# Softcap attention and a max-out feed-forward on one core: a new order of work up to the ninth quad, and hand-overs placed anew

## The chip, the core and the metric

The kernel runs on one core of a Trainium2 chip. The metric is the device time of one execution in microseconds (us), given as the median of several runs. The engines that matter are TensorE (PE, with its weight loads as PEld), VectorE (DVE), ScalarE (ACT), GpSimd (POOL) and SyncE (SP). Each engine takes its instructions one after the other from its own queue and meets the others by semaphores. Here POOL issues most of the loads, SP the stores and the transposing loads, so a wait on one of these queues holds back the transfers that are queued behind it.

## The reference

```python
# q, k, v: (8, 12, 448, 64) float32; cap = 30
scores = scale * np.matmul(q, k.transpose(0, 1, 3, 2))   # scale = 1/8
scores = cap * np.tanh(scores / cap)
attn = softmax(scores)
x = (attn @ v).transpose(0, 2, 1, 3).reshape(3584, 768)
# w1, w2: (768, 1024); w_out: (1024, 768)
h1 = x @ w1
h2 = x @ w2
out = np.maximum(h1, h2) @ w_out                          # (3584, 768) float32
```

Each of 8 batches has 12 heads over 448 tokens. The scores are squeezed by a tanh, made into weights by an exponential and a division by their sum, and applied to the values. The result, heads side by side, is the input of a feed-forward layer that takes the larger of two projections.

## The kernel before

**What is computed where.** A *pair* is two heads, a *quad* t is the pairs 2t and 2t+1; there are 24 quads, three to a batch. All products are in bf16. For each pair PE computes the scores, keys by queries, in three steps of 128 keys (`S i j`, line 514) into one of two PSUM tiles that are used in turn; the 64 keys that remain of each head are done for a quad at once (`L t`, line 528). ACT takes the tanh out of PSUM (`T i j`, line 519; `TL t`, line 532) and later the exponential in SBUF (`E i j0 j1`, line 536; `EL t`, line 539). Since tanh bounds the scores by 30, no maximum is subtracted. The sums over keys are made by PE with a matrix of ones (`Y t`, lines 566, 570 and 573); from the fourth quad on DVE first adds the key blocks (`A`, line 548, and `B`, line 553), so that PE has fewer matmuls to do. DVE inverts the sums (`Y1`, `Y2`, `Y3`, lines 578, 581, 584), PE applies the values (`VL t`, line 600, for the leftover keys, which opens the sum, then `V t u j0 j1`, line 606), which land in a score tile too, and DVE multiplies by the inverse and writes the input of the layer, `xT` (`N t u`, lines 618 and 621).

**The layer.** The larger of two projections is x·w2 + relu(x·(w1−w2)). So the kernel forms wd = w1−w2 once (`sub c e`, line 402, on DVE or POOL) and wm = w2·w_out once: PE transposes w2 (`W`, line 416, copied out by `WC`, line 420) and multiplies (`OP c half bank` opens a sum in a bank, `P c half n` adds n of its 8 matmuls, line 431, `PC` copies it out on DVE, line 437). Then every stage 1 group computes gT = relu(wd·x) for 128 of the 1024 columns of one batch, and every stage 2 group x·wm + gT·w_out for 128 tokens and half of the 768 columns, in 14 units. There are 120 groups. `O g bank` opens one in one of four PSUM banks; a unit is a matmul of 128 rows, done as two half matmuls of 64 rows that may run beside each other in the upper and the lower half of PE's rows. `M x y n` issues n pairs: the upper half of group x's next unit and the lower half of group y's (line 645). So a group is finished in two spells, one in each row half, and neighbouring groups overlap.

**Hand-overs.** Both halves of a group add into the same bank. When a group goes from one row half to the other, the first matmul there waits for a nop, which itself waits for the group's last matmul in the first half: `H g` puts the nop on DVE, `Hs g` on SP (line 654). As DVE and SP are queues, what stands behind such a nop waits with it. Of 145 such passes in the kernel before, 107 have a nop on SP, 21 one on DVE and 17 none.

**Evictions and stores.** `ev g` empties a finished group on DVE (relu at line 666, copy at line 702), `eva g` does the copy on ACT (line 700); `st b t` stores on SP (lines 676 to 681, 705 to 707).

**Loads and transposes.** `ld0` and `cd` load and cast the first pair's rows; `lk`, `lq`, `lv`, `lw1`, `lw2`, `lwo` are loads issued by POOL that cast on the way (lines 321, 328, 352, 393, 366, 360). The first ten pairs are transposed by PE (`X i bank`, `Xh`, line 458, copied by `XC`, line 463), the later quads by a transposing transfer issued by SP (`cr t`, line 475). `D bank n` is a filler matmul on PE while nothing else can run (line 471).

**What sets the order.** The program is one list of steps, `ORDER`, written out from line 9 on; a loop at the end calls each step's function, and the instructions go to their engines in this sequence. Nothing is rescheduled: moving a step in the list moves its instructions on its engine past the others of that engine.

```python
for s in ORDER.split(";"):
    if s.strip():
        name, *args = s.split()
        STEPS[name](*[int(a) if a.lstrip("-").isdigit() else a for a in args])
```

Of the kernel before, what the change touches and what calls it, by code (L numbers as in the profile page):

```python
# [24 lines left out]
OP 5 1 3; P 5 1 4; S 6 2; L 3; Y 2 1; T 6 2; TL 3; E 6 0 3; VL 2; V 2 1 0 1; V 2 0 0 3; V 2 1 1 3; S 7 0; P 5 1 4;
OP 5 0 0; P 5 0 8; Y1 2; Y2 2; Y3 2; N 2 0; N 2 1; A 3 0 1; A 3 0 2; PC 5 1; PC 5 0; T 7 0; EL 3; lk 9 0; lq 11 0;
lv 3 1; lq 9 0; lw1 1; lw1 3; lq 10 0; lk 12 1; lv 3 0; lw1 5; lk 10 0; lk 11 0; lk 11 1; lk 10 1; S 7 2; O 0 1;
M 0 -1 2; S 7 1; M 0 -1 4; O 1 2; M 1 -1 1; T 7 2; T 7 1; Hs 0; M 1 -1 1; S 8 1; M 1 -1 1; M 1 0 3; S 8 0; X 9 3;
OP 4 1 0; P 4 1 4; sub 1 0; sub 3 0; XC 9; T 8 1; E 7 0 2; T 8 0; E 7 2 3; P 4 1 4; L 4; O 2 3; M 2 0 3; S 8 2;
M 2 1 3; A 3 1 1; B 3 1; PC 4 1; ev 0; B 3 0; Hs 2; TL 4; T 8 2; O 3 0; M 3 1 3; M 3 2 1; S 9 0; M 3 2 2; T 9 0;  # L30
E 8 0 3; ev 1; A 3 1 2; sub 5 0; cr 5; Hs 3; O 4 1; M 4 2 1; VL 3; V 3 0 0 3; Y 3 2; V 3 1 0 3; M 4 2 2; S 9 1;
M 4 3 3; lk 13 0; lk 13 1; lv 4 1; lv 4 0; lv 5 3; lv 5 0; lq 13 0; lq 15 0; lq 12 0; lk 12 0; lk 15 1; Y1 3;
Y2 3; Y3 3; ev 2; Hs 4; O 5 2; M 5 3 3; M 5 4 3; T 9 1; EL 4; ev 3; N 3 0; N 3 1; Hs 5; O 6 3; M 6 4 3; M 6 5 2;
S 10 0; M 6 5 1; O 7 0; M 7 5 3; Hs 6; ev 4; A 4 0 1; ev 5; M 7 6 2; S 9 2; M 7 6 1; Hs 7; cr 6; E 9 0 2; T 10 0;
T 9 2; O 8 1; M 8 6 3; S 10 2; M 8 7 3; S 10 1; O 9 2; M 9 7 1; T 10 2; T 10 1; E 9 2 3; M 9 7 2; VL 4; V 4 0 0 2;
L 5; TL 5; A 4 1 1; H 8; A 4 0 2; B 4 1; ev 7; B 4 0; A 4 1 2; ev 6; M 9 8 3; V 4 1 0 3; Y 4 0; V 4 0 2 3;
M 9 8 7; S 11 0; M 9 8 1; O 10 3; M 10 8 3; E 10 0 3; T 11 0; EL 5; Hs 9; Hs 8 2; Y1 4; M 10 9 3; Y2 4; Y3 4;
N 4 1; N 4 0; M 8 9 2; S 11 1; M 8 9 3; S 11 2; M 8 9 3; lv 5 2; lk 15 0; lk 14 0; lv 6 1; lk 14 1; lq 14 0;
lv 5 1; lq 16 0; lv 6 3; lv 6 0; lk 16 1; lk 17 0; lk 16 0; T 11 1; T 11 2; E 11 0 2; O 11 0; M 11 9 3; S 12 0;
M 11 10 6; S 12 1; M 11 10 1; ev 8; ev 9; A 5 0 1; A 5 0 2; lk 17 1; M 11 10 4; T 12 0; lq 17 0; O 12 1;  # L40
M 12 10 1; A 5 1 1; M 12 10 1; Hs 11; cr 7; M 12 10 1; M 12 11 1; B 5 0; M 12 11 1; T 12 1; M 12 11 1; S 12 2;
# [164 lines left out]
def kernel(  # L206
# [21 lines left out]
    P = 128  # L228
# [550 lines left out]
```

## Time and profile before

| what | value |
|---|---|
| median of 3 runs | 328.49 us (328.19 to 328.52) |
| span of the profiled execution | 326.9 us |
| time of the profiled execution beside its span | not given on the page; the median lies 1.59 us above the span |
| PE busy | 320.2 us, 98%, 4138 matmuls |
| ACT busy | 281.1 us, 86%, 278 instructions |
| DVE busy | 240.1 us, 73%, 422 instructions |
| POOL busy | 162.2 us, 50% |
| chain that ended last | PE 93%, DMA 3%, POOL 1%, DVE 1% |

The span runs from the first to the last instruction of the profiled execution. Busy time of an engine counts every moment in which one of its instructions is under way; matmuls overlap, so that a PE that is busy all the time may still start its matmuls further apart than it could. The chain of waits is followed back from the last instruction. In a row of a group the name at the left of the arrow is what is written and at the right what is read; behind x stands the count, then the busy time and the mean length of one in ns, then the idle time ahead of them and what ended it. In a row of a timeline stand the start, the length, the engine, the line and the number of instructions that were merged into the row.

### The profile page before, as it was taken

Reading aid. Unit: us, or ns where it says so; the run is one execution under the profiler, and the core shown is the slowest. Engines: PE = TensorE matmul, PEld = TensorE weight load, DVE = VectorE, ACT = ScalarE, POOL = GpSimd, SP = SyncE. Lnnn points to the kernel's source line nnn. Section 1 sums busy time; section 2 is a strip of 40 time slices with the busy share of each in tenths; the row PEclk is TensorE's granted clock in tenths of the full one; section 3 lists DMA queues with packets and bytes.
Section 4 is the critical chain, followed back from the end, with each engine's and each line's share of the span. In section 5 each row is a group of like instructions: output and inputs, shape, how many; then the busy total and the mean of one; then the engine's idle time right before and its main releaser. Section 6 shows DMA issues by size and latency. Waiting matters only on the chain.

```text
span 326.9 us, 9772 instructions
## 1 busy us (share of the span) xinstructions
PE 320.2 (98%) x4138; PEld 184.5 (56%) x4138; DVE 240.1 (73%) x422; ACT 281.1 (86%) x278; POOL 162.2 (50%) x237
## 2 busy tenths in 40 slices
PE   7999999999999999999999999999999999999994
PEld 3454545545656664565565565556466556557662
DVE  3346899987997778987897788968878779773201
ACT  5999999999999999999999999999999999921120
POOL 7357584568772772764774474478448311000000
PEclk9999999999999999999999999999999999999999
DMA  8999999899999999999999999999999963013033
GB/s 179 174 202 185 269 256 112 92 140 116 221 188 98 134 182 191 102 99 175 163 176 108 208 114 181 128 140 182 183 116 101 201 156 45 2 50 98 0 98 96
DMA packets 134508, 46.28 MB, mean 142 GB/s; under 512 B 112321, under 2 KB 129473, under 8 KB 134465
## 3 DMA queue, kind: packets, MB, share of 16 engines
q0 software_dynamic: 94592, 25.02, 78.3%
q1 hardware_dynamic: 39424, 19.99, 31.1%
q8 instruction: 32, 0.52, 0.6%
q10 hardware_dynamic: 448, 0.66, 0.5%
q14 instruction: 12, 0.09, 0.1%
HBM read 47.78 MB, written 11.01 MB: 180 GB/s over the span
## 4 chain that ended last, share of the span: by engine, by line
PE 93%; DMA 3%; POOL 1%; DVE 1%; issue 0%
PE mm L645 61%; PE s L514 9%; PE s L606 9%; PE mm L431 5%; DMA w2b<-in_moe_w_dram 3%; PE s L528 2%; PE s L600 2%; PE mm L573 2%; PE mm L640 1%; POOL kqs L321 1%; PE mm L458 1%; PE mm L566 1%; PE mm L416 0%; DVE xT L621 0%; POOL w2b L366 0%; DVE xT L618 0%
## 5 line engine op out<-in xcount | busy, mean ns | idle before, releaser
L519 ACT ACTIVATE e<-s 128x896 bf16<-128x896 f32 x144 | 125.5, 927 | 5.7 <-PE s L514 5.2
L536 ACT ACTIVATE e<-e 128x1792 bf16<-128x1792 bf16 (+2 forms) x72 | 122.7, 1709 | 0.0
L645 PE MATMUL mm<-wo_sb,gT 64*128 64x384 bf16 x864 | 115.2, 323 | 0.0
L645 PE MATMUL mm<-wm_sb,xT 64*128 64x384 bf16 x648 | 102.2, 323 | 0.0
L645 PE MATMUL mm<-xT,wd_sb 64*128 64x448 bf16 x768 | 97.5, 349 | 0.0
L328 POOL DMA_DIRECT2D kqs<-in_k_dram x76 | 54.7, 722 | 56.1 <-DMA qkT<-kqs 50.9
L645 PEld LDWEIGHTS <-gT 64*128 64x128 bf16 x864 | 58.6, 94 | 25.5 <-issue 1.1
L645 PEld LDWEIGHTS <-wd_sb 64*128 64x128 bf16 x768 | 48.8, 94 | 26.7 <-issue 2.1
L645 PEld LDWEIGHTS <-xT 64*128 64x128 bf16 x648 | 50.3, 94 | 18.5 <-issue 0.2
L514 PE MATMUL s<-qkT 64*128 64x448 bf16 x288 | 52.7, 352 | 0.2 <-DVE xT L618 0.2
L352 POOL DMA_DIRECT2D vp<-in_v_dram x48 | 30.5, 639 | 32.6 <-PE s L514 23.5
L666 DVE TENSOR_SCALAR gT<-mm 128x448 bf16<-128x448 f32 x64 | 38.9, 617 | 8.7 <-PE mm L645 7.6
L328 POOL DMA_DIRECT2D kqs<-in_q_dram x38 | 35.1, 924 | 5.7 <-issue 2.5
L606 PE MATMUL s<-e,vp 128*32 128x448 bf16 x576 | 36.1, 354 | 0.0
L548 DVE TENSOR_TENSOR esum<-e 128x896 bf16<-128x896 bf16 x42 | 25.9, 617 | 9.1 <-ACT e L536 9.1
L621 DVE TENSOR_TENSOR xT<-s,inv 64x448 bf16<-64x448 f32 x48 | 29.9, 622 | 1.7 <-PE s L606 0.8
L548 DVE TENSOR_TENSOR esum<-esum,e 128x896 bf16<-128x896 bf16 x42 | 26.2, 623 | 5.9 <-ACT e L536 4.8
L514 PEld LDWEIGHTS <-qkT 64*128 64x128 bf16 x288 | 18.5, 94 | 20.1 <-issue 12.0
L700 ACT COPY osb<-mm 128x384 f32<-128x384 f32 x10 | 4.8, 479 | 26.9 <-PE mm L645 26.7
L702 DVE COPY osb<-mm 128x384 f32<-128x384 f32 x44 | 23.3, 554 | 6.2 <-PE mm L645 5.7
L553 DVE TENSOR_TENSOR esum<-esum,el 64x896 bf16<-64x896 bf16 x42 | 26.0, 619 | 1.2
L578 DVE STREAM_TRANSPOSE st<-mm 128x448 f32<-128x448 f32 x24 | 15.6, 649 | 13.0 <-PE mm L573 11.3
(57 smaller groups left out, 269.7 us busy)
## 6 DMA issues: line engine op xcount, KB each, us to landing
out_dram<-osb SPq DMA_DIRECT2D x54, 192.0 KB, 4.5
vp<-in_v_dram POOLq DMA_DIRECT2D x38, 160.0 KB, 4.3
kqs<-in_q_dram POOLq DMA_DIRECT2D x46, 112.0 KB, 5.8
kqs<-in_k_dram POOLq DMA_DIRECT2D x76, 56.0 KB, 4.4
osb<-in_moe_w_dram POOLq DMA_DIRECT2D x4, 512.0 KB, 7.4
w2b<-in_moe_w_dram POOLq DMA_DIRECT2D x6, 256.0 KB, 7.1
wo_sb<-in_moe_w_out_dram POOLq DMA_DIRECT2D x4, 384.0 KB, 9.9
vp<-in_v_dram POOLq DMA_DIRECT2D x10, 128.0 KB, 7.7
```

The lines of the kernel that those rows point to most:

```text
L328: nc.gpsimd.dma_start(out=to, in_=x)
L352: nc.gpsimd.dma_start(out=to, in_=x)
L514: scored[i, j] = nc.tensor.matmul(s[:, h, :S], k_of(t, o, h, j), q_of(t, o, h)).ins
L519: nc.scalar.activation(expo[i][:, 2 * j : 2 * j + 2, :], slots[i, j][:, :, :S], AF.Tanh, scale=scale / cap)
L536: nc.scalar.activation(e, e, AF.Exp, scale=float(cap))
L548: nc.vector.tensor_add(d, e[:, 0:2, :] if j == 1 else d, e[:, 2 * j : 2 * j + 2, :])
L553: nc.vector.tensor_add(d, d, left_e[t][r, :, :])
L606: nc.tensor.matmul(vals[t][place(m, u), u, :S], w[:, m, :], expo[2 * t + o][:, 2 * j + h, :], start=False, stop=(j == NJ - 1))
L621: nc.vector.tensor_mul(x[64 - r : 128 - r], vals[t][r : r + 64, u, :S], sums[t, 3][64 - r : 128 - r])
L645: ins = nc.tensor.matmul(self.ps, w[r], x[r], start=first, stop=self.at == [self.n, self.n]).ins
L666: nc.vector.tensor_relu(gT[b // 2][:, f, cs], ps)
L702: nc.vector.tensor_copy(o[:, hs], ps)
```

## The change

The list of steps is written anew; the functions stay, but for one condition in `transposes`. All steps keep their number, except that the filler steps `D` make one matmul less. In detail:

- POOL issues its loads in the same sequence as before. First loads and casts keep their sequence on each engine.
- From the second pair on: the tanh `T 2 0` comes ahead of pair 1's exponentials, `S 2 2` ahead of the premultiplication; the steps `P` of blocks 1, 2 and 3 alternate in small portions; `Y 0`, the sums of the first quad, come ahead of `VL 0` and `X 4`; `X 7` comes ahead of `X 6`, `S 5 1` ahead of `S 5 2`, `S 7 1`, `S 7 2` and `X 9` ahead of the first `M` steps of a single half. The exponentials of pairs 7, 11, 15 and 17 stand elsewhere between the tanh steps. Up to the ninth quad `M`, `P` and `S` alternate in another way.
- From step `L 10` on, PE has the same sequence of matmuls.
- Each of the 145 passes between row halves now has a hand-over: 90 on SP, 55 on DVE, most of them at other places in the list. Between them the places of `cr`, `st`, `ev` and of DVE's other steps shift on SP and DVE.
- The evictions of groups 10, 25, 27 and 29 go from DVE (`ev`) to ACT (`eva`).
- In `transposes` a bank is opened whenever one is given, where before it was when the second half wasn't asked for alone; no instruction changes by it.

The core of the diff (the list of steps is some 200 lines on each side):

```diff
@@ -7,197 +7,205 @@
 ORDER = """
...
-S 1 1; D 0 8; D 2 2; S 2 1; W 1 2; WC 2; WC 1; T 1 1; T 2 1; S 2 0; D 0 4; L 1; OP 3 0 0; P 3 0 2; OP 1 0 1;
-P 1 0 4; P 3 0 2; OP 2 0 3; P 2 0 7; P 1 0 1; P 2 0 1; P 1 0 1; P 3 0 2; P 1 0 2; PC 2 0; PC 1 0; E 1 2 3;
-E 1 0 2; TL 1; T 2 0; EL 0; S 3 0; S 2 2; P 3 0 1; W 0 2; P 3 0 1; X 4 3; T 2 2; T 3 0; VL 0; Y 0 1; V 0 0 0 3;
...
-S 5 0; X 6 0; E 4 0 3; T 5 0; EL 2; Y1 1; Y2 1; PC 2 1; Y3 1; N 1 1; N 1 0; XC 6; X 7 2; W 4 1; S 5 2; S 5 1;
-X 8 0; P 3 1 3; WC 4; XC 8; PC 3 1; T 5 1; T 5 2; OP 4 0 1; P 4 0 2; OP 0 1 0; P 0 1 3; S 6 0; S 6 1; W 5 3;
...
-M 7 6 2; S 9 2; M 7 6 1; Hs 7; cr 6; E 9 0 2; T 10 0;
-T 9 2; O 8 1; M 8 6 3; S 10 2; M 8 7 3; S 10 1; O 9 2; M 9 7 1; T 10 2; T 10 1; E 9 2 3; M 9 7 2; VL 4; V 4 0 0 2;
-L 5; TL 5; A 4 1 1; H 8; A 4 0 2; B 4 1; ev 7; B 4 0; A 4 1 2; ev 6; M 9 8 3; V 4 1 0 3; Y 4 0; V 4 0 2 3;
...
-M 27 26 1; T 18 1; M 27 26 1; S 18 2; ev 25; M 27 26 2; T 18 2; M 27 26 1; B 8 0; M 27 26 4; B 8 1; st 1 3;
...
-M 64 62 1; ev 61; M 64 62 1; Hs 63; EL 16; M 64 62 1;
-S 33 1; lv 17 3; N 15 1; M 64 63 3; T 33 1; lk 38 1; O 65 1; M 65 63 2; Hs 64; M 65 63 1; M 65 64 1; ev 62;
...
+S 1 1; WC 2; lv 1 1; T 1 1; S 2 1; D 0 8; T 2 1; S 2 0;
+W 1 1; T 2 0; L 1; WC 1; E 1 2 3; S 2 2; OP 1 0 1; P 1 0 2; OP 2 0 2; P 2 0 1; TL 1; P 1 0 1; OP 3 0 3; P 3 0 1;
+P 1 0 1; P 3 0 1; P 2 0 1; EL 0; P 2 0 2; P 3 0 2; P 1 0 1; T 2 2; P 1 0 1; P 3 0 1; P 2 0 2; P 3 0 1; E 1 0 2;
+P 1 0 2; P 3 0 1; P 2 0 2; S 3 0; PC 2 0; W 0 0; T 3 0; PC 1 0; Y 0 2; WC 0; E 2 0 3; S 3 1; Y1 0; VL 0; X 4 1;
+Y2 0; V 0 1 0 3; lk 8 0; XC 4; V 0 0 0 3; Y3 0; lq 8 0; T 3 1;
...
+X 7 1; X 6 0; lq 11 0; P 3 1 1; T 5 0; P 3 1 1; N 1 0; P 3 1 2; W 4 2; lv 3 1; EL 2; XC 6; S 5 1; lq 9 0; XC 7;
+S 5 2; T 5 1; X 8 0; lw1 1; WC 4; P 3 1 2; T 5 2; XC 8;
...
+M 7 6 2; A 4 1 1; T 9 2; M 7 6 1; S 10 2; H 7; O 8 1; M 8 6 1; A 4 0 1; lk 12 0; M 8 6 2;
+T 10 2; M 8 7 1; ev 5; S 10 1; lk 15 1; M 8 7 2; B 4 0; T 10 1; VL 4; lv 5 2; V 4 0 0 2; A 4 0 2; E 9 2 3;
+lk 15 0; L 5; Hs 8; B 4 1; O 9 2; M 9 7 2; TL 5; lk 14 0; M 9 7 1; A 4 1 2; M 9 8 3; ev 7; cr 6; M 9 8 1;
...
+H 24; T 18 1; M 26 25 1; lk 23 0; M 26 25 2; st 1 3; M 24 25 2; E 17 0 2; lk 23 1; M 24 25 4; lq 23 0; H 26;
+M 24 25 2; S 18 2; O 27 3; M 27 25 2; T 18 2; M 27 25 1; M 27 26 1; A 8 1 1; M 27 26 3; eva 25; B 8 0;
...
+ev 61; EL 16; M 64 62 1; Hs 63; S 33 1; M 64 63 1; N 15 1; lk 38 0; M 64 63 2; T 33 1; O 65 1; M 65 63 2;
+lv 17 0; M 65 63 1; Hs 64; M 65 64 1; ev 62; S 33 2; lv 17 1; S 34 0; M 65 64 1; T 33 2; ev 63; M 65 64 1;
...
@@ -445,7 +453,7 @@
     def transposes(i, bank, c=None):
 
-        if c != 1:
+        if bank is not None:
             turned["qk", i] = mm_tile(bank).bitcast(bf16)
```

More of the change, by code (lines that the diff above doesn't have):

```diff
@@ L25 @@
[L25 to L29, printed above, removed]
@@ new lines @@
+VL 2; Y1 2; lk 10 1; V 2 1 0 1; V 2 1 1 3; E 6 0 3; Y2 2; V 2 0 0 3; Y3 2; O 0 1; M 0 -1 1; S 7 0; N 2 1;
+OP 5 0 0; P 5 0 3; P 5 1 3; T 7 0; P 5 0 1; N 2 0; P 5 0 1; P 5 1 1; P 5 0 2; A 3 0 1; EL 3; P 5 0 1; S 7 1;
+sub 1 0; S 7 2; T 7 1; X 9 2; M 0 -1 1; lk 13 0; M 0 -1 1; T 7 2; XC 9; M 0 -1 2; S 8 0; A 3 0 2; lk 13 1;
+M 0 -1 1; E 7 0 2; O 1 2; M 1 -1 1; Hs 0; M 1 -1 1; PC 5 0; S 8 1; lv 4 1; M 1 -1 1; sub 3 0; M 1 0 2; lv 4 0;
+M 1 0 1; P 5 1 1; T 8 1; OP 4 1 0; P 4 1 1; lv 5 3; P 4 1 1; Hs 1; A 3 1 1; P 4 1 3; T 8 0; PC 5 1; P 4 1 3;
@@ new lines @@
+M 15 14 2; T 14 0; lq 18 0; Hs 15; O 16 1; M 16 14 1; A 6 1 1; M 16 14 2; M 16 15 1; T 14 1; B 6 1; M 16 15 1;
+lk 19 0; S 14 2; M 16 15 1; ev 14; O 17 2; M 17 15 1; T 14 2; M 17 15 1; lk 19 1; st 0 1; Hs 16; M 17 15 1;
+B 6 0; M 17 16 2; E 13 2 3; M 17 16 1; lq 19 0; L 7; ev 15; VL 6; cr 8; V 6 1 0 2; TL 7; A 6 1 2; H 17;
+V 6 0 0 2; V 6 1 2 3; E 14 0 3; Y 6 0; V 6 0 2 3; Y1 6; O 18 3; M 18 16 1; lv 8 0; M 18 16 2; S 15 0; Y2 6;
+M 18 17 1; lv 8 1; ev 16; M 18 17 2; Hs 18; O 19 0; M 19 17 1; lv 8 2; Y3 6; M 19 17 1; st 0 2; M 19 17 1;
@@ new lines @@
+H 28; M 30 29 2; M 28 29 4; H 30; T 20 1; M 28 29 1; A 9 1 1; M 28 29 2; st 1 5; M 28 29 1; O 31 0; M 31 29 1;
+T 20 2; M 31 29 1; ev 28; M 31 29 1; M 31 30 1; B 9 0; M 31 30 1; eva 29; M 31 30 1; O 32 1; M 32 30 1; H 31;
+M 32 30 1; B 9 1; E 19 2 3; M 32 30 1; L 10; VL 9; ev 30; TL 10; V 9 0 0 2; A 9 1 2; V 9 1 0 2; E 20 0 3;
+M 32 31 1; Y 9 3; V 9 0 2 3; V 9 1 2 3; Y1 9; S 21 0; M 32 31 2; Y2 9; O 33 3; M 33 31 1; Hs 32; Y3 9;
+M 33 31 2; lk 26 0; M 33 32 1; T 21 0; M 33 32 1; N 9 0; M 33 32 1; O 34 2; M 34 32 1; Hs 33; lv 11 0;
@@ new lines @@
+M 38 39 1; lq 28 0; M 38 39 1; cr 13; A 11 0 2; M 38 39 1; T 23 2; O 41 1; M 41 39 1; S 24 0; M 41 39 1; ev 38;
+M 41 39 1; lk 29 0; M 41 40 1; E 23 0 2; M 41 40 1; ev 39; S 24 1; M 41 40 1; lk 29 1; M 41 40 4; st 2 0;
+lq 29 0; M 41 40 2; T 24 0; M 41 40 1; A 11 1 1; M 41 40 1; H 41; O 42 2; M 42 40 3; T 24 1; H 40; B 11 0;
+M 42 41 1; S 24 2; M 42 41 2; B 11 1; M 40 41 1; T 24 2; M 40 41 3; H 42; M 40 41 2; E 23 2 3; M 40 41 2;
+O 43 0; M 43 41 1; ev 40; L 12; VL 11; A 11 1 2; TL 12; V 11 0 0 2; V 11 1 0 2; E 24 0 3; Y 11 3; V 11 0 2 3;
@@ new lines @@
+B 13 0; S 28 2; M 53 52 2; T 28 2; O 54 2; M 54 52 1; H 53; M 54 52 1; B 13 1; M 54 52 1; M 54 53 2; E 27 2 3;
+Hs 52; M 54 53 1; M 52 53 1; L 14; VL 13; TL 14; V 13 0 0 2; A 13 1 2; V 13 1 0 2; Hs 54; E 28 0 3; Y 13 0;
+V 13 0 2 3; V 13 1 2 3; Y1 13; S 29 0; M 52 53 1; lk 34 0; M 52 53 1; Y2 13; M 52 53 2; Y3 13; M 52 53 2;
+lv 15 0; M 52 53 1; O 55 0; M 55 53 1; N 13 0; M 55 53 2; T 29 0; lv 15 1; M 55 54 2; N 13 1; M 55 54 2;
+lv 15 2; EL 14; M 55 54 2; S 29 1; lv 15 3; M 55 54 2; T 29 1; M 55 54 1; ev 52; S 29 2; lk 34 1; M 55 54 1;
@@ new lines @@
+cr 17; M 58 59 1; H 60; A 15 1 1; M 58 59 1; lk 37 1; M 58 59 3; T 32 1; B 15 0; M 58 59 1; lq 37 0; S 32 2;
+O 61 1; M 61 59 1; ev 58; M 61 59 1; T 32 2; M 61 59 1; M 61 60 1; B 15 1; M 61 60 2; E 31 2 3; O 62 2;
+M 62 60 1; ev 59; M 62 60 1; st 3 5; M 62 60 1; L 16; ev 60; VL 15; TL 16; H 61; V 15 0 0 2; A 15 1 2;
+V 15 1 0 2; st 3 6; E 32 0 3; M 62 61 1; Y 15 0; V 15 0 2 3; V 15 1 2 3; Y1 15; S 33 0; M 62 61 2; Y2 15;
+O 63 3; M 63 61 1; Hs 62; Y3 15; M 63 61 2; M 63 62 1; T 33 0; M 63 62 1; N 15 0; M 63 62 1; O 64 0; M 64 62 2;
@@ new lines @@
+M 75 74 2; ev 73; M 75 74 1; Hs 75; T 38 0; O 76 0; M 76 74 1; lq 43 0; A 18 1 1; M 76 74 1; cr 20; M 76 74 1;
+M 76 75 1; T 38 1; B 18 0; S 38 2; M 76 75 2; H 76; O 77 1; M 77 75 1; ev 74; T 38 2; M 77 75 2; B 18 1;
+M 77 76 1; E 37 2 3; M 77 76 2; st 4 2; ev 75; O 78 3; M 78 76 1; L 19; VL 18; A 18 1 2; TL 19; V 18 0 0 2;
+V 18 1 0 2; E 38 0 3; Hs 77; Y 18 2; V 18 0 2 3; V 18 1 2 3; Y1 18; S 39 0; lv 20 0; M 78 76 2; Y2 18;
+M 78 77 1; Y3 18; M 78 77 1; lv 20 1; M 78 77 1; O 79 2; M 79 77 2; ev 76; lv 20 2; M 79 77 1; T 39 0; Hs 78;
@@ new lines @@
+M 86 84 1; T 41 2; M 86 84 1; H 85; S 42 0; A 20 0 1; lk 47 0; M 86 84 1; M 86 85 2; E 41 0 2; A 20 0 2;
+M 86 85 1; lk 47 1; H 86; S 42 1; Hs 84; M 84 85 1; cr 22; M 84 85 2; lq 47 0; M 84 85 5; T 42 0; O 87 2;
+M 87 85 1; A 20 1 1; M 87 85 2; M 87 86 1; ev 84; T 42 1; M 87 86 2; S 42 2; st 5 3; ev 85; M 87 86 2; T 42 2;
+M 87 86 1; B 20 0; M 87 86 4; B 20 1; E 41 2 3; M 87 86 1; O 88 0; M 88 86 2; st 5 4; L 21; VL 20; A 20 1 2;
+TL 21; V 20 0 0 2; V 20 1 0 2; E 42 0 3; Y 20 1; V 20 0 2 3; Hs 87; V 20 1 2 3; Y1 20; S 43 0; lv 22 0;
@@ new lines @@
+M 95 94 1; ev 92; S 45 2; S 46 0; M 95 94 1; T 45 2; ev 93; M 95 94 1; O 96 0; M 96 94 2; Hs 95; A 22 0 1;
+M 96 94 1; E 45 0 2; M 96 95 1; S 46 1; ev 94; M 96 95 2; O 97 3; M 97 95 1; A 22 0 2; Hs 96; M 97 95 2;
+M 97 96 1; T 46 0; M 97 96 1; ev 95; M 97 96 1; O 98 1; M 98 96 2; A 22 1 1; M 98 96 1; T 46 1; Hs 97;
+M 98 97 1; S 46 2; B 22 0; M 98 97 2; T 46 2; O 99 2; M 99 97 1; ev 96; M 99 97 1; Hs 98; M 99 97 1; M 99 98 1;
+E 45 2 3; B 22 1; M 99 98 3; L 23; ev 97; VL 22; TL 23; V 22 0 0 2; A 22 1 2; V 22 1 0 2; E 46 0 3; Y 22 0;
@@ new lines @@
+V 22 0 2 3; V 22 1 2 3; Y1 22; S 47 0; M 99 98 2; Y2 22; M 99 98 2; Y3 22; M 99 98 3; O 100 3; M 100 98 1;
+N 22 0; M 100 98 1; Hs 99; M 100 98 1; T 47 0; M 100 99 2; N 22 1; Hs 98; M 100 99 1; M 98 99 1; EL 23;
+M 98 99 2; S 47 1; M 98 99 2; H 100; T 47 1; M 98 99 1; A 23 0 1; S 47 2; M 98 99 2; A 23 0 2; O 101 0;
+M 101 99 1; T 47 2; M 101 99 2; M 101 100 1; ev 98; M 101 100 2; E 47 0 2; M 101 100 1; ev 99; M 101 100 7;
+O 102 1; M 102 100 2; Hs 101; E 47 2 3; st 6 0; M 102 100 1; A 23 1 1; M 102 101 3; B 23 0; H 100; VL 23;
```

316 lines of the change are left out of this document (139 added, 177 removed).

## The prediction

> **What bounds the kernel now.** I read the page first (span, busy shares, chain), then the windows view over stretches, then the groups of lines of the first stretch, then timelines of single engines. The page:
>
> ```profile
> span 326.9 us, 9772 instructions
> PE 320.2 (98%) x4138; PEld 184.5 (56%) x4138; DVE 240.1 (73%) x422; ACT 281.1 (86%) x278; POOL 162.2 (50%) x237
> PE 93%; DMA 3%; POOL 1%; DVE 1%; issue 0%
> ```
>
> PE carries the chain for 93% of the span, so a change of order can win only what PE loses between its matmuls. The runs' median of 328.49 lies 1.59 above this span; I take that 1.59 as unchanged and count inside the span.
>
> The change rewrites the order up to about quad 10 (step L 10, at 124.71) and behind that moves hand-overs, evictions and DMA issues, while PE's sequence stays. So I compare PE in two stretches: from the first P to L 10, and from L 10 to L 16 (columns: window, length, busy us and counts of PE, PEld, DVE, ACT, POOL, clock, then two on DMA; the middle row serves further below).
>
> ```profile
> 16.77:124.71 107.94, 107.76 (x1427) 60.69 (x1428) 88.58 (x152) 106.00 (x103) 69.12 (x99) 1.00 1.32 168
> 40.00:72.00 32.00, 32.00 (x389) 15.97 (x387) 31.13 (x51) 31.72 (x32) 19.74 (x27) 1.00 1.23 151
> 124.71:195.04 70.33, 70.33 (x922) 41.15 (x921) 58.12 (x103) 68.42 (x67) 42.77 (x60) 1.00 1.36 151
> ```
> ```profile
> 124.71 0.38 PE L528 MATMUL s<-qkT 64*32 64x448 bf16 x8
> 124.91 0.37 PE L600 MATMUL s<-el,vl 64*32 64x448 bf16 x8
> ```
>
> By busy time PE loses 0.18 us in the first stretch (107.94 less 107.76) and nothing in the second. But a matmul's row is longer than the distance to the next start, as these rows of the chain and of PE's timeline show:
>
> ```profile
> 16.77 3.75 PE mm L431 x22
> 100.44 0.32 PE L645 MATMUL mm<-wm_sb,xT 64*128 64x384 bf16 x1
> 100.60 0.32 PE L645 MATMUL mm<-wm_sb,xT 64*128 64x384 bf16 x1
> 103.14 0.55 PE L606 MATMUL s<-e,vp 128*32 128x448 bf16 x8
> 103.62 0.37 PE L514 MATMUL s<-qkT 64*128 64x448 bf16 x2
> 103.82 0.32 PE L645 MATMUL mm<-wo_sb,gT 64*128 64x384 bf16 x1
> ```
>
> Twenty-two matmuls of 384 columns take 3.75: (3.75−0.33)/21 = 0.163 from start to start, and 0.16 between the two of line 645. I use 0.1625, and 0.189 for 448 columns (two rounds of four in 0.55: 0.55−0.36). From 103.14 two rounds take 0.38, the next starts at 103.62: 0.10 for the switch of tile shape. From 103.62 to 103.82, without a switch, there is one pitch. Eight L or VL matmuls take 0.20 (124.71 to 124.91). Now PE's work in the first stretch can be counted in starts:
>
> ```profile
> L645 PE MATMUL mm<-wo_sb,gT 64*128 64x384 bf16 x224 | 30.5, 323 | 0.0
> L645 PE MATMUL mm<-xT,wd_sb 64*128 64x448 bf16 x213 | 28.6, 349 | 0.0
> L645 PE MATMUL mm<-wm_sb,xT 64*128 64x384 bf16 x168 | 26.9, 323 | 0.0
> L514 PE MATMUL s<-qkT 64*128 64x448 bf16 x110 | 20.4, 352 | 0.2 <-DVE xT L618 0.2
> L431 PE MATMUL mm<-wo_sb,w2T 128*128 128x384 bf16 x96 | 17.3, 327 | 0.0
> L606 PE MATMUL s<-e,vp 128*32 128x448 bf16 x216 | 13.3, 354 | 0.0
> L458 PE MATMUL mm<-ident,kqs 64*64 64x64 bf16 x168 | 3.6, 194 | 0.0
> L528 PE MATMUL s<-qkT 64*32 64x448 bf16 x64 | 3.1, 360 | 0.0
> L573 PE MATMUL mm<-esum,ones 128*32 128x448 bf16 x24 | 2.5, 353 | 0.0
> L566 PE MATMUL mm<-e,ones 128*32 128x448 bf16 x36 | 2.3, 356 | 0.0
> L600 PE MATMUL s<-el,vp 64*32 64x448 bf16 x40 | 2.0, 360 | 0.0
> L416 PE MATMUL mm<-ident,w2b 128*128 128x128 bf16 x24 | 1.9, 220 | 0.0
> L600 PE MATMUL s<-el,vl 64*32 64x448 bf16 x32 | 1.5, 349 | 0.0
> L570 PE MATMUL mm<-el,ones 128*32 128x448 bf16 x12 | 1.1, 352 | 0.0
> ```
>
> Two row halves run side by side: M (224+168)/2×0.1625 = 31.85 and 213/2×0.189 = 20.13; S 110/2×0.189 = 10.40; P 96×0.1625 = 15.60; V 216/4×0.189 = 10.21; X, six steps of 28 at 0.455 ((0.63−0.19)/27 each, the row at 37.08 below), 2.73; L and VL (64+72)/8×0.20 = 3.40; Y 72/4×0.189 = 3.40; W 24×0.056 = 1.34 ((0.62−0.22)/7, the row at 15.20 below). That is 99.06, and with 57 switches of shape, counted in the order, 104.76. **PE loses 3.2 us of 107.94.** From L 10 to L 16 the code gives 392 and 192 halves of M, 72 S, 144 V, 48 L, 48 VL, 24 Y: 67.1, and with 20 switches 69.1 of 70.33, so 1.2 lost (1.7%). A wrong pitch would sit in both, so the difference between the stretches is safer than either. At the steady rate the first would lose 1.8: **about 1.4 us lie there for a better order.**
>
> [...]
>
> **The change part by part.** *Warm-up and first loads.* D loses one matmul of 4138, the issues of POOL keep their sequence, and casts and first loads keep their order on each engine. PE waits there for a transfer:
>
> ```profile
> 15.20 0.62 PE L416 MATMUL mm<-ident,w2b 128*128 128x128 bf16 x8 [0.52 <-DMA w2b<-in_moe_w_dram]
> 15.55 2.59 ACT L536 ACTIVATE e<-e 128x896 bf16<-128x896 bf16 x2
> 18.78 0.99 ACT L519 ACTIVATE e<-s 128x896 bf16<-128x896 f32 x1
> 21.04 1.73 ACT L519 ACTIVATE e<-s 128x896 bf16<-128x896 f32 x2 [0.44 <-PE s L514]
> ```
>
> That wait (W 1) stays, for the transfer doesn't move: nothing won or lost. D's are filler in front of it.
>
> *T 2 0 ahead of the exponentials, S 2 2 ahead of P.* T 2 0 moves from 18.78 to about 15.6. S 2 2 then needs its tile, free at about 16.5, so P begins about 0.1 later than at 16.77: +0.1. Bounds: 0, if T 2 0 ends at 16.4, and +0.3, if it starts one cast later. What it gives is on ACT: the idle 0.44 before 21.04 goes, and two tanh in 1.73 (0.80 from start to start) follow 0.6 to 0.9 earlier. ACT is busy 106.00 of 107.94 in this stretch, so this lead lets PE run ahead to about 65 us.
>
> *Y 0 sooner, VL 0 and X 4 behind S 3 1.* The first sums need only E and EL 0; DVE's inverses and N 0 come sooner. X 4 ends about 1.0 later (Y 0 0.57, S 3 1 0.19, VL 0 0.20); lk 8, the load that reuses its buffer, is issued later by as much, and behind it on POOL's queue all later loads. They are issued many quads ahead of their use, so I cost it at nothing; without that lead it is one late S, bounded by 1.0.
>
> *P's of blocks 1 to 3 interleaved, S 5 1 before S 5 2, X 7 before X 6, S 7 and X 9 between M's.* The same 96 P's, no more switches (59 against 57, 0.2, of which 0.19 comes back as one S pair leaves the stretch). The wait that these can remove is seen here:
>
> ```profile
> 35.87 0.62 DVE L618 TENSOR_TENSOR xT<-s,inv 128x448 bf16<-128x448 f32 x1
> 36.55 0.55 PE L514 MATMUL s<-qkT 64*128 64x448 bf16 x4 [0.16 <-DVE xT L618]
> 37.08 0.63 PE L458 MATMUL mm<-ident,kqs 64*64 64x64 bf16 x28
> ```
>
> S 5 2 follows W 4 and waits for N 1 0's end at 36.49; in the new order P's and W 4 lie between. This is 0.2 to 0.3 of the 1.4; the rest are pieces of 0.1 to 0.2 from 33 to 90 us. I take −1.4, with ends 0 (every piece has a successor) and −3.2.
>
> *New waits.* Following the new order by hand, with these pitches, PE comes to VL 2 (score tile of T 6 2) 0.12 early, to S 9 0 0.07 and S 9 2 0.15 early, since ACT is busy with two exponentials (2.59 for two E's). Together +0.34; ends 0 and +1.0.
>
> *Evictions 10, 25, 27, 29 from DVE to ACT.*
>
> ```profile
> L700 ACT COPY osb<-mm 128x384 f32<-128x384 f32 x10 | 4.8, 479 | 26.9 <-PE mm L645 26.7
> L702 DVE COPY osb<-mm 128x384 f32<-128x384 f32 x44 | 23.3, 554 | 6.2 <-PE mm L645 5.7
> DVE esum L548 <- ACT e L536: 3.7, 4, 1.1
> ```
>
> ACT gets 4×0.48 = 1.9 us more, DVE 2.2 less. From L 10 to L 16 ACT has 1.9 free in 70.33, in the first stretch 1.9 too. The first of them is paid from ACT's lead; the other three fall at 80 to 100 us, a quad apart, with 0.3 of slack each. Behind each waits the next tanh, and PE's S after that. I cost them at 0, with ends 0 and 4×0.48 = +1.9.
>
> *Hand-overs.* A nop on DVE or SP waits for the last matmul of a group's one half before the other half may start. Before, 107 on SP, 21 on DVE and 17 passes without one; now 90, 55, none. The one round trip that the trace of before shows bare is at the end, over SP:
>
> ```profile
> 315.20 0.65 PE L645 MATMUL mm<-wo_sb,gT 64*128 64x384 bf16 x3
> 315.94 0.33 PE L645 MATMUL mm<-wo_sb,gT 64*128 64x384 bf16 x1
> ```
>
> There group 116 has its last matmul in one half at 315.20+2×0.16 = 315.52 and its first in the other at 315.94: 0.42. Most passes have four pairs between, 4×0.1625 = 0.65, so 0.23 to spare; followed by hand, none gets late in the unchanged part on an idle DVE. I take 0, with ends −1.2 (all that the steady part loses there) and the slower rival's +1.6. But a nop on DVE stands in DVE's line: in front of it may be an operation of 0.62, or an add that waits for ACT. DMA issues on SP that now stand behind an Hs (cr 8 behind Hs 16) start later by the wait of that Hs, at most some pairs of 0.1625; the transposes are used quads later (S 16 for cr 8): 0. Others (cr 12, cr 18) move ahead of one.
>
> Sum: 328.49 + 0.1 − 1.4 + 0.34 = **327.5 us** (−0.3%).
>
> **Rivals.** *Slower: DVE's line holds hand-overs.* 34 more passes go over DVE. The wait row above shows adds held by ACT for up to 1.1 us. A hand-over behind one 0.62 operation comes up to 0.62−0.23 = 0.39 late, and so does PE. Four such on top of the forecast give 327.5+1.6 = 329.1; from three late ones on the gain of 1.0 is gone. For it: DVE is busy 88.58 of 107.94, and 31.13 of the 32.00 from 40 to 72 us. Against: most moved ones stand right before an eviction that has to wait for PE anyway. Chance 0.25. [...]
>
> *No change: PE waits for ACT elsewhere.* ACT's 106.00 plus 1.9 of evictions equals the stretch of 107.94; if PE only arrives sooner at the same tanh, the 1.4 becomes waits before S: 328.4. For it: ACT's idle before tanh is small already. Against: the lead of 0.6 to 0.9 at the start. Chance 0.23.
>
> *Larger gain.* The hand-overs also remove some of the 1.2 per 70 us, or more than 1.4 of the 3.2 goes: 328.49−2.5 = 326.0. Chance 0.1.
>
> **How the numbers follow.** The forecast has 0.42. 0.2% (0.66 us; the runs shown differ by 0.33) is about what can be told from no change. The forecast's own range is 326.9 to 328.0. Faster 0.42+0.1 less a little that falls inside 0.2%: 0.5; within 0.24; slower 0.26. The range for 8 in 10 reaches from 326.3, most of the larger gain, to 329.5, just past four late hand-overs.
>
> **What would show it.** Right: P starts at 16.85; T 3 0 near 21.2 instead of 21.8; no wait of PE at S 5; L 10 starts at 123.7 to 123.9; L 16 and the end follow by the same shift. Wrong: PE idle before M with DVE as releaser between 50 and 72 us (slower rival); S waiting for ACT at 80 to 100 us behind an eviction on ACT (no change); the distance L 10 to L 16 other than 70.3 (hand-overs matter in the steady part, either way).

## The result, and the profile after

The changed kernel takes 330.26 us in the median of 7 runs (328.94 to 331.98), against 328.49 for the kernel before (327.87 to 329.73 over 7 runs). The ratio is 1.0054, with a 95% interval of 1.0037 to 1.0071: slower by half a per cent where 0.3% faster was forecast, and outside the range that was given. The runs of the changed kernel also lie three microseconds apart, those before within two. The ratios below are those on record, which can differ from the quotient of two medians by up to 0.0014. In one of the later series a run of old_new_old took 656.36 us and one of the kernel before 832.05 us; both count as slow and are left out of the ratios.

The page of the changed kernel, which in its profiled execution took 329.74 us around a span of 328.0:

```profile
span 328.0 us, 9789 instructions
...
PE 320.6 (98%) x4135; PEld 184.5 (56%) x4137; DVE 239.0 (73%) x418; ACT 282.9 (86%) x282; POOL 161.6 (49%) x237
...
PE 91%; ACT 3%; DMA 3%; DVE 1%; issue 1%; DVEq 0%
```

PE's busy time is nearly that of before (320.2), and no other engine became the bound. PE carries 91% of the chain instead of 93%. The stretches from the first P to L 10, L 10 to L 16 and L 16 to L 22 (columns as in the prediction):

```profile
16.82:125.09 108.27, 107.80 (x1427) 60.34 (x1425) 86.64 (x148) 107.33 (x107) 68.26 (x99) 1.00 1.34 169
125.09:195.80 70.71, 70.60 (x923) 41.31 (x922) 58.62 (x103) 68.73 (x67) 42.63 (x60) 1.00 1.30 148
195.80:266.44 70.64, 70.64 (x922) 41.17 (x921) 58.40 (x103) 68.43 (x67) 38.14 (x54) 1.00 1.37 153
```

The first stretch takes 108.27 instead of 107.94, where 106.9 was expected, and each of the two steady ones 0.3 to 0.4 more than the 70.33 of before, though PE has the same matmuls in the same order there. So this execution loses 0.33 in the part that was rewritten and 0.69 behind it, together 1.02 of its 1.1.

**Where PE stands.** PE's idle is counted here from starts, with the prediction's pitches (a pitch is the time from one start to the next): the length of a stretch, less a pitch for each matmul and 0.10 for each switch of shape. The stretches are cut at the starts of the leftover steps; L 3, L 7 and L 9 start at 42.82, 89.51 and 113.17 before and at 42.59, 89.01 and 112.74 in the changed kernel. In us:

| stretch | before | changed |
|---|---|---|
| P to L 3 | 0.64 | 0.61 |
| L 3 to L 7 | 2.10 | 1.76 |
| L 7 to L 9 | 0.20 | 0.90 |
| L 9 to L 10 | 0.14 | 0.14 |
| L 10 to L 14 | 1.00 | 1.11 |
| L 14 to L 22 | 1.38 | 1.96 |

From L 3 to L 7 the new order wins 0.34, although just ahead of L 7 PE stands and waits for the hand-over of group 16. From L 7 to L 9 0.70 is lost again, and behind L 10 another 0.69. The waits by engine and releaser (us in total, times, longest), and PE's timeline at one of those places, in the changed kernel:

```profile
PEld L522 <- DMA qkT<-kqs: 0.7, 1, 0.7
PEld L653 <- SPq L662: 0.6, 2, 0.4
...
PE s L522 <- DMA qkT<-kqs: 0.3, 1, 0.3
```
```profile
97.64 0.37 PE L522 MATMUL s<-qkT 64*128 64x448 bf16 x2 [0.27 <-DMA qkT<-kqs]
```

The trace of before has no such rows. Line 662 is the hand-over (line 654 before), and SPq is SP's queue: matmuls and their weight loads wait for a nop on SP. The scores at 97.64 are S 16 0, which wait for the transposing load cr 8. SP's timeline around it, in the changed kernel and then before:

```profile
86.45 1.79 SPq L689 DMA_DIRECT2D out_dram<-osb  x2
88.61 2.52 SPq L483 DMA_TRANSPOSE qkT<-kqs  x1
```
```profile
87.20 1.75 SPq L475 DMA_TRANSPOSE qkT<-kqs  x1
```

The store st 0 1 occupies SP for 1.79 from 86.45; the hand-over of group 16, behind it, is released at 88.30 by the trace's semaphore events, 1.15 after its matmul started where the usual is 0.37 to 0.41, and PE takes it 0.05 later. Only then comes cr 8, at 88.61 instead of 87.20. It lands 8.98 later, at 97.6. The time that an issue occupies SP is itself no constant. In the views of the tiles qkT and osb of the changed kernel (columns: count, then shortest, median and longest in ns, then first and last start):

```profile
L483 SPq DMA_TRANSPOSE qkT<-kqs x19: 1296/1717/2802, 52.0 to 260.7; - x19
```
```profile
L689 SPq DMA_DIRECT2D out_dram<-osb x46: 466/588/1327, 78.1 to 320.2; - x46
```

A store step has two of the second kind. With 0.23 to spare per pass (the prediction's estimate, 0.65 less 0.42), a hand-over that has to wait behind either for most of its length would be late.

### The profile page after: what moved, and what is told of

The parts are those of the page before. It is cut to its first block, busy times and chain, and to the rows that moved or that the text cites. A ratio compares the mean times of both kernels' runs of the same rounds, so it can differ in the third digit from the quotient of the medians.

```text
span 328.0 us, 9789 instructions
## 1 busy us (share of the span) xinstructions
PE 320.6 (98%) x4135; PEld 184.5 (56%) x4137; DVE 239.0 (73%) x418; ACT 282.9 (86%) x282; POOL 161.6 (49%) x237
## 4 chain that ended last, share of the span: by engine, by line
PE 91%; ACT 3%; DMA 3%; DVE 1%; issue 1%; DVEq 0%
PE mm L653 58%; PE s L522 9%; PE s L614 9%; PE mm L439 5%; DMA qkT<-kqs 3%; PE s L536 2%; ACT e L527 2%; PE mm L581 2%; PE s L608 2%; PE mm L466 2%; PE mm L648 1%; PE mm L479 1%; ACT e L544 1%; PE mm L574 1%; PE mm L424 0%
## 5 line engine op out<-in xcount | busy, mean ns | idle before, releaser
L708 ACT COPY osb<-mm 128x384 f32<-128x384 f32 x14 | 6.7, 480 | 26.9 <-PE mm L653 26.7
L561 DVE TENSOR_TENSOR esum<-esum,el 64x896 bf16<-64x896 bf16 x42 | 26.0, 618 | 1.8 <-PE mm L653 0.6
L710 DVE COPY osb<-mm 128x384 f32<-128x384 f32 x40 | 21.2, 554 | 3.4 <-PE mm L653 2.9
```

The lines of the kernel that those rows point to most:

```text
L561: nc.vector.tensor_add(d, d, left_e[t][r, :, :])
L710: nc.vector.tensor_copy(o[:, hs], ps)
```

## The experiments

Two theories stand against each other. **Queue theory:** the loss comes from single places where a hand-over, or what stands behind one, is held in a queue: cr 8 and the hand-over of group 16 in the first part, a few others behind L 10. **First-part theory:** the new first part itself is worse and the rest is neutral. As smaller rivals stand the four evictions on ACT and the many nops on DVE. "Before" below is the median of the runs of the kernel before in the same series.

### The two halves

```
new_start:  the changed list up to L 10, then the steps of before's list that are left
new_rest:   the list of before up to L 10, then the steps of the changed list that are left
```

> The changed kernel up to the step L 10, the list of before from there on (its hand-overs, evictions, DMA issues). Queue theory (hand-over nops hold DVE's line in the steady part, and one transposing load, cr 8, and one hand-over on SP come late in the first part): L 10 starts 0.4 later than in the profile of before (124.7), from L 10 to L 22 it takes 140.7 as before, and the time is 0.7 below that of the changed kernel. First-part theory (all of the loss lies in the new first part, the rest is neutral): the time of the changed kernel, 330.3, and L 10 about 1.8 late.

> The kernel before up to L 10, the changed list from there on. Queue theory: L 10 at 124.7, from L 10 to L 22 141.35 instead of 140.66, with the new waits at S 31 2, Y 18 and Y 10, so about 329.2. First-part theory: 140.7 from L 10 to L 22 and 328.5.

new_start took 328.62 (before 328.36; ratio 1.0013, 0.9984 to 1.0042), with one of ten runs at 332.42. new_rest took 329.12 (ratio 1.0028, 1.0015 to 1.0041). So the rest costs 0.76 with PE's order unchanged, as the queue theory has it, and the first-part theory, by which it costs nothing, falls. new_start is 0.9 below what even the queue theory expected: with the rest of before behind it, the new first part costs 0.26 in the median, and its interval holds no change. The two costs add up to 1.02 of the 1.77; these two runs don't show where the other 0.75 is, but the interval of new_start reaches to 1.0042, which is 1.4 us. In new_start's profiled execution, with cr 8 in the same late place, no transposing load takes more than 8.2 from issue to landing (6.5 in the median), and no scores wait for one. The profiled execution of new_rest shows the queue at work:

```profile
159.85 0.93 PE L653 MATMUL mm<-xT,wd_sb 64*128 64x448 bf16 x7 [0.98 <-SPq L662]
```
```profile
156.02 3.72 SPq L483 DMA_TRANSPOSE qkT<-kqs  x1
```

The hand-over of group 46 stands behind cr 14 on SP. In this execution cr 14's issue took 3.72, up to 159.74, and PE stood still for 0.98; from L 10 to L 22 it took 142.34 instead of the 141.35 that was expected. In the profiled execution of the changed kernel the issue took 2.79, and the same hand-over was in time. So the same hand-over, behind the same load, cost PE 0.98 in one profiled execution and nothing in the other; that issue times are the reason for the changed kernel's spread is not shown.

### cr 8 and the hand-over of group 16

```diff
-lk 19 1; st 0 1; Hs 16;
+lk 19 1; cr 8; st 0 1; H 16;
...
-VL 6; cr 8; V 6 1 0 2;
+VL 6; V 6 1 0 2;
```

> The changed kernel with cr 8 ahead of the store st 0 1 on SP, and the hand-over of group 16 on DVE instead of behind that store. Queue theory: the waits before S 16 0 (0.5) and before group 16's second half (0.24) go, L 10 starts at 124.4 to 124.6, the time falls by 0.5 to 0.7 and the spread between runs gets smaller. Rival (the transposing load is late because its own transfer is slow, not because of its place): S 16 0 still waits 0.4 or more and the time stays within 0.2.

329.58 (before 328.36; ratio 1.0034, 1.0019 to 1.0050): 0.68 below the changed kernel, as expected. The two intervals overlap, so this step by itself isn't clear of the noise. The counted idle from L 3 to L 9 falls from 2.66 to 1.86, and the waits for cr 8 and group 16 are gone from the trace. L 10 starts at 124.09, sooner than expected: another 0.4 is missing ahead of L 3, where this execution doesn't have a stop that is described further below. The spread (328.45 to 330.36) is two thirds of what it was.

### What a nop on DVE costs, and what one on SP

```diff
 H 31; L 10; ...
-Hs g        (80 places in before's list)
+H g
```

> The kernel before with its 80 hand-overs on SP from L 10 on put on DVE, at the same places in the list. Queue theory: DVE stops at each nop until PE has done the group's last matmul in its first half, and N and A behind it come late; 18 more of them on DVE in the changed kernel go with 0.7, so 80 should cost 1 to 4 us: 329.5 to 332.5. Rival (a nop on DVE costs nothing, since DVE is idle 15 to 20% of the time there): 328.5, within 0.3.

329.00 (before 328.36; ratio 1.0017, 1.0006 to 1.0029), less than the queue theory and more than the rival expected. In its profiled execution L 10 to L 22 takes 140.89 instead of 140.66, and from there to the end 61.9 instead of 61.5: about 0.6 for 80 nops, under 0.01 each. So nops on DVE as such cost little, though not nothing. In the changed kernel's trace no matmul of the layer waits for a nop on DVE; the slower rival of the prediction, put generally, falls.

```diff
-H g         (16 places in before's list: H 31, just ahead of L 10, and 15 behind it)
+Hs g
```

> The kernel before with its 16 hand-overs on DVE from L 10 on put on SP at the same places in the list, so that those behind a transposing load or a store stand behind its issue. Queue theory: those of groups 46, 53, 61 and their like come 0.3 to 1.5 us late in most executions, the time rises by 1 to 4 us and its spread with it. Rival (an issue on SP holds a hand-over no longer than 0.2 us): 328.4, within 0.3.

330.31 (before 328.66; ratio 1.0045, 1.0030 to 1.0060). Sixteen nops moved from DVE to SP cost 1.65, about what the whole change costs. The waits, and the timelines of PE and SP at group 46:

```profile
PE mm L645 <- SPq L654: 1.2, 2, 0.9
```
```profile
PEld L645 <- SPq L654: 2.9, 4, 1.3
```
```profile
160.50 0.93 PE L645 MATMUL mm<-xT,wd_sb 64*128 64x448 bf16 x7 [0.88 <-SPq L654]
```
```profile
157.83 2.56 SPq L475 DMA_TRANSPOSE qkT<-kqs  x1
```

Four hand-overs come late: those of groups 38, 46, 68 and 76 (of the three that were named ahead, 46 alone). PE goes on behind the one of 46 at 160.50, 0.11 after cr 14's issue has left SP (157.83+2.56 = 160.39). The rival, that an issue holds a hand-over no longer than 0.2, falls.

### Three more places

```diff
-M 35 33 1; Hs 34; M 35 33 1; M 35 34 1;
+M 35 33 1; H 34; M 35 33 1; M 35 34 1;
...
-ev 44; M 47 45 1; Hs 46; st 2 2;
+ev 44; M 47 45 1; H 46; st 2 2;
...
-M 76 75 2; H 76; O 77 1; M 77 75 1; ev 74; T 38 2;
+M 76 75 2; O 77 1; M 77 75 1; ev 74; H 76; T 38 2;
```

> The kernel with cr 8 ahead, and three more single places changed: the hand-over of group 34 on DVE instead of behind the store st 1 6 on SP, that of group 46 on DVE instead of behind cr 14 on SP, and the one of group 76 on DVE behind the eviction ev 74 instead of ahead of it. Queue theory: the passes of 34 and 46 are no longer late (they came 0.05 us before their use, after 0.8 and 1.1 to 2.0 us of waiting), Y 18 starts its second half 0.2 sooner, and the time falls from 329.6 to 329.0 (0.3 to 1.0 lower), with less spread. Rival (the late passes are harmless chance, the loss is spread thinly over all of the new places): within 0.2 of 329.6.

On top of cr8_ahead this gives 328.54 (before 328.66; ratio 1.0005, 0.9989 to 1.0020): of the 1.77 that the change cost, nothing is left that can be told from noise, and the interval lies clear below that of the changed kernel. The spread, 328.09 to 330.45, did not get smaller than cr8_ahead's, as was expected. The third place is the one that stands on DVE. DVE's timeline in the changed kernel and with the four places changed:

```profile
228.93 0.62 DVE L561 TENSOR_TENSOR esum<-esum,el 64x896 bf16<-64x896 bf16 x1
229.87 0.62 DVE L674 TENSOR_SCALAR gT<-mm 128x448 bf16<-128x448 f32 x1 [0.32 <-PE mm L653]
...
231.83 0.62 DVE L556 TENSOR_TENSOR esum<-esum,e 128x896 bf16<-128x896 bf16 x1
```
```profile
228.02 0.62 DVE L561 TENSOR_TENSOR esum<-esum,el 64x896 bf16<-64x896 bf16 x1
228.56 0.61 DVE L674 TENSOR_SCALAR gT<-mm 128x448 bf16<-128x448 f32 x1
...
230.51 0.63 DVE L556 TENSOR_TENSOR esum<-esum,e 128x896 bf16<-128x896 bf16 x1
```

In the changed kernel DVE is idle for 0.32 ahead of the eviction at 229.87: there stands the nop of group 76, which waits for PE. The eviction, two more operations and the addition at 231.83 all follow that much later, and the second half of Y 18 needs this addition. From the one operation at L561 to the addition it takes 2.90 in the changed kernel and 2.49 in the other; the counted idle from L 18 to L 22 falls from 0.83 to 0.57. It is a DVE operation late behind a nop, and not a nop late behind a DVE operation.

```
new_rest_three_places:  before's list up to L 10, then the changed list with these three places
```

> The kernel before up to L 10, the changed list from there on, with the three places of that part changed as in four_places (hand-overs of groups 34 and 46 on DVE, that of 76 behind ev 74). Queue theory: these three places carry the 0.76 that the changed rest cost: 328.4 to 328.7, level with before. Rival (the loss is spread over all of the rest's new places): 329.0 or more.

328.83 (before 328.46; ratio 1.0013, 1.0004 to 1.0021), between what the two theories expected. The cost of the rest falls from 0.76 to 0.37: the three places carry about half of it. What the other 0.37 is, its profiled execution doesn't settle: its counted idle from L 10 to L 22 is 2.56, against 2.38 before.

### The evictions

```diff
-eva 10;  eva 25;  eva 27;  eva 29;
+ev 10;   ev 25;   ev 27;   ev 29;
```

> The changed kernel with the evictions of groups 10, 25, 27 and 29 back on DVE. Queue theory: no part in it, within 0.3 of the changed kernel's 330.26. Eviction theory (four copies of 0.48 us on ACT delay the tanh and so PE's scores at 80 to 125 us): 0.5 to 1.9 lower, with the waits of S for ACT gone.

330.89 (before 328.66; ratio 1.0054, 1.0037 to 1.0071). The ratio is that of the changed kernel to the fourth digit, but the median lies 0.63 above 330.26, where within 0.3 was expected. Taking the four copies off ACT wins nothing, so the eviction theory falls. In its profile one wait is new, that of the sums Y 5 for the eviction of group 10, now on DVE:

```profile
PE mm L581 <- DVE osb L710: 0.3, 1, 0.3
```

### cr 8 alone, in the kernel before

```diff
-M 16 14 1; st 0 1; M 16 14 1; Hs 15; T 14 1; cr 8; B 6 0;
+M 16 14 1; M 16 14 1; Hs 15; T 14 1; B 6 0;
...
-M 17 15 2; H 16; M 17 15 1;
+M 17 15 2; st 0 1; Hs 16; M 17 15 1;
...
-L 7; VL 6;
+L 7; VL 6; cr 8;
```

> The kernel before with one group of steps on SP as the change has it: st 0 1, then the hand-over of group 16 (on SP, not DVE), then cr 8 behind VL 6. Queue theory: the pass of group 16 comes 0.25 late behind the store's issue, S 16 0 waits for cr 8's transfer, together 0.5 to 0.9 slower: 329.0 to 329.5. Rival (the place of cr 8 costs nothing, as the prediction took it, since its use lies a quad away): 328.5, within 0.2.

328.68 (before 328.62; ratio 1.0013, 0.9990 to 1.0035): the median doesn't show it, which is the rival's answer. But one run of ten took 332.42, and it is the one with the profile:

```profile
85.65 0.36 PE L514 MATMUL s<-qkT 64*128 64x448 bf16 x2 [0.62 <-DMA qkT<-kqs]
...
95.14 1.31 PE L645 MATMUL mm<-xT,wd_sb 64*128 64x448 bf16 x11 [0.24 <-SPq L654]
...
99.90 0.36 PE L514 MATMUL s<-qkT 64*128 64x448 bf16 x2 [1.56 <-DMA qkT<-kqs]
```

There cr 8 is issued at 90.31 and lands 9.54 later. It costs 1.56 before S 16, and a hand-over 0.24 (the 0.62 at S 14 is cr 7, which wasn't moved). So what the late places on SP cost is a matter of chance here: nine of the ten runs took 328.18 to 329.27, the one with an issue of 3.41 and a landing after 9.54 took 332.42. Why cr 8 takes 8.98 to land in the profile of the changed kernel, 9.54 here and no more than 8.2 in that of new_start, all three from the late place, stays open.

### The new order without its queues

```
best_of_both:     cr8_ahead's list up to L 10, then before's
old_new_old:      before's list up to L 3, four_places' up to L 10, then before's
old_new_old_l8:   before's list up to L 3, four_places' up to L 8, then before's
```

> The changed list with cr 8 ahead up to L 10, the list of before from there on. Queue theory: the first part wins what its order gives (0.5 less of PE's idle up to L 10 than before), and nothing is lost behind it: 327.8 to 328.1, so faster than the kernel before by 0.1% to 0.2%. First-part theory (the new order gives nothing): 328.4 or more.

> The list of before up to L 3 (42.8 us), then that of four_places up to L 10, then before again. Queue theory: the counted waits fall by 0.5 to 0.6 between L 3 and L 9 (0.7 won from L 3 to L 8, 0.2 lost behind Y 7), none are added: 327.9 to 328.2. Rival (what the new order wins between L 3 and L 8 is only PE's lead, given back at the next wait): 328.4 to 328.7.

> As old_new_old, but back to the list of before from L 8 on, so that Y 7's wait for DVE's last addition is left out as well. Queue theory: 0.2 lower than old_new_old, 327.7 to 328.0. Rival: 328.4 to 328.7.

best_of_both took 329.08 (before 328.66; ratio 1.0008, 0.9996 to 1.0020): a miss, the new first part as a whole gives nothing. old_new_old took 328.28 (before 328.62; ratio 0.9989, 0.9979 to 0.9999), just above what was expected. old_new_old_l8 took 327.72 (ratio 0.9975, 0.9965 to 0.9985), as expected; its interval lies below no change, a quarter of a per cent faster than the kernel before, and it has the smallest spread of all (327.44 to 328.12). It is 0.56 below old_new_old, where 0.2 was expected. Its page and stretches:

```profile
span 325.8 us, 9776 instructions
```
```profile
16.24:123.58 107.34, 107.16 (x1435) 61.23 (x1427) 88.09 (x151) 106.35 (x105) 68.77 (x99) 1.00 1.30 169
123.58:193.91 70.33, 70.33 (x921) 41.15 (x920) 58.14 (x103) 68.38 (x67) 42.67 (x60) 1.00 1.24 147
```

The first stretch takes 0.60 less than before, and the steady one is back at 70.33. Its counted idle from L 3 to L 8 is 1.65, against 2.25 in the kernel before. The other 0.5 of its shorter span is an earlier first P (16.24 against 16.77), which is luck: with the old start P hangs on W 1, and W 1 waits 0.52 for its transfer in the profile of the kernel before, 1.13 in that of before_nops_on_dve and not at all here.

That the new list from L 8 to L 10 loses 0.2 is seen in Y 7, which takes 0.59 in the changed kernel and 0.36 before, since its second half waits for DVE's addition of 101.85 to 102.48. The changed kernel's rows, and then that of before:

```profile
101.85 0.63 DVE L556 TENSOR_TENSOR esum<-esum,e 128x896 bf16<-128x896 bf16 x1
```
```profile
102.30 0.59 PE L581 MATMUL mm<-esum,ones 128*32 128x448 bf16 x4
```
```profile
102.95 0.36 PE L573 MATMUL mm<-esum,ones 128*32 128x448 bf16 x4
```

That the new list up to L 3 is worse by 0.8 (best_of_both against old_new_old, from two series) isn't explained. From the first P to L 10 the two profiled executions take the same, 107.54 and 107.63, so what is lost would lie ahead of P, or be chance between the series. What the profiles do show of this list is a stop of 0.3 to 0.5 in X 6, in four of the six profiles that have it, for which the profile names no cause. In the changed kernel:

```profile
33.91 1.04 PE L466 MATMUL mm<-ident,kqs 64*64 64x64 bf16 x53
35.15 0.24 PE L466 MATMUL mm<-ident,kqs 64*64 64x64 bf16 x3 [0.20 <-issue]
```

## Why the prediction was wrong

**The step that failed** is the one on hand-overs, "I take 0", and with it the last sentence of that part, that DMA issues on SP behind or ahead of an Hs cost 0. It priced what a hand-over costs on an idle engine (0.42; measured 0.37 to 0.41 from the start of the matmul to the nop, and 0.05 more to PE: right) and looked for late ones on DVE alone. On SP, with 90 hand-overs, it saw no rival. There an issue occupies the queue for 0.5 to 1.3 per store transfer in the changed kernel's profile and for 1.3 to 3.7 per transposing load over all profiles, against 0.23 to spare. new_rest puts what the rest costs at 0.76, four_places takes 1.7 off the whole with one late load and four hand-overs (three of them late on SP, and one that held DVE), and before_nops_on_sp makes 1.65 out of the engine of 16 nops alone. The forecast was 0.96 below the kernel before and the result is 1.77 above it: of the 2.7 between them, 1.7 stand at these places and 1.0 is the gain that did not come. The sign that the prediction had named for this, a distance from L 10 to L 16 other than 70.3, came out: 70.71.

**The slower rival** had the direction and the wrong place: a nop late behind a DVE operation cost PE nothing that the changed kernel's trace shows, and 80 more nops on DVE cost about 0.6 together. The reverse, an addition late behind a nop at group 76, was not thought of.

**cr 8 at 0** was wrong by about 0.45 in the changed kernel's profiled execution. "The transposes are used quads later" is true of the list but not of the clock: PE came to S 16 0 at about 97.2, 8.6 us after the issue, and the transfer took 8.98.

**The 1.4 that lay there for a better order** was mis-sized. The mechanism is right: PE's idle behind overlapping rows can be counted from starts, and the new order takes 0.6 of it away between L 3 and L 8 (old_new_old_l8). But 0.25 is lost again at Y 7, and ahead of L 3 the stop in X 6 takes back 0.3 to 0.5 where it occurs. The wait of S 5 2 is gone, as forecast.

**New waits of 0.34** at VL 2, S 9 0 and S 9 2 don't show in the changed kernel's trace; the ones that came are at X 6, Y 7 and S 16 0. **The evictions at 0**: evictions_on_dve bears it out, within its interval. **The no-change rival by ACT**: in the changed kernel's trace matmuls wait for ACT once, the 0.36 before S 2 2, so this cause is excluded there. Its 328.4 didn't follow from its own terms either: without the −1.4 the sum is 328.49 + 0.1 + 0.34 = 328.9.

**The warm-up at 0** came out, but by luck. W 1 starts at 15.22 instead of 15.20, yet it no longer waits for its transfer; in its place the scores S 2 1 wait for 0.44, which the profile puts down to DVE's copy of w2T. **The first P, +0.1**, and T 3 0 near 21.2 are right in this profile: P starts at 16.82, behind S 2 2's wait for its tile, and T 3 0 at 21.14. Counted from PE's first transposition of w2, P comes 4.85 to 4.87 later in all six profiles with the new start, and 4.06 to 5.24 later, 4.55 in the median, in the eight with the old one. So on average it is rather +0.3. The changed kernel's rows:

```profile
14.09 0.36 PE L522 MATMUL s<-qkT 64*128 64x448 bf16 x2 [0.44 <-DVE w2T L428]
15.22 0.62 PE L424 MATMUL mm<-ident,w2b 128*128 128x128 bf16 x8
16.52 0.36 PE L522 MATMUL s<-qkT 64*128 64x448 bf16 x2 [0.36 <-ACT e L527]
```

Busy time alone doesn't show the gain: by it PE loses 0.18 in the first stretch before (107.94 less 107.76) and 0.18 in old_new_old_l8 as well (107.34 less 107.16), and yet the stretch is 0.60 shorter.

## What to carry to other kernels

When a semaphore nop is put on a queue, price what stands ahead of it there in its longest case, not its median: an issue of a transposing load took 1.7 us in the median of the changed kernel and 3.7 at the longest over all profiles, which makes a nop behind it a lottery. Don't put a nop ahead of work that could already run (here the nop of group 76 went behind an eviction instead of ahead of it), and issue long transfers ahead of the nops. If a new order gains in one stretch and the whole gets slower, splice the two lists at steps that both have: the part that gains can be kept.

## What was not expected of the hardware

The time that the issue of a transposing load occupies SP's queue varies between 1.30 and 3.72 us over the profiles, though all these loads have one size, and cr 14's alone was 2.79 in one and 3.72 in another. In the traces of before and of the changed kernel a hand-over whose queue is free takes 0.37 to 0.41 from the start of a matmul of 384 or 448 columns to the nop on either engine, and 80 nops moved from SP to DVE cost about 0.6 us in all (before_nops_on_dve).
